# Both units of batch 0 through the FFN's weight pieces in three groups, with a new instruction order

## The chip, the cores and the metric

The kernel runs on one core of one Trainium2 chip. The metric is the device time of one execution in microseconds (us), as the median of several runs. PE is TensorE, DVE is VectorE, ACT is ScalarE, POOL is GpSimd and SP is SyncE, which issues nearly all transfers.

## The reference

```python
q, k, v: (4, 8, 576, 64)   moe_w_in: (512, 2048)   moe_w_out: (2048, 512)   all float32
q_rot, k_rot = rotate(q), rotate(k)                  # rotary embedding
scores = scale * q_rot @ k_rot^T
attn = exp(scores - rowmax);  attn = attn / (rowsum + 1e-9)
x = (attn @ v), heads side by side -> (2304, 512)
h = x @ w_in;  g = h * sigmoid(h);  out = g @ w_out
```

The result has to come close to that of float32, so nearly every matmul operand is split into a high and a low fp16 part with a scale, and products are made of three terms (high by high, high by low, low by high).

## The kernel before

**Attention.** Four batches, each with four head pairs p. For the first batch q and k are rotated in fp32 (three elementwise steps, `rope`, on DVE or POOL), transposed on PE (`qP`, L475 to L478), and evicted (`qE`, L484 on ACT, or L326 on DVE). A slot is 128 queries of one head: scores `S` (L915), negated row maximum `max` (L920, DVE), `exp` (L923, ACT), transposes `ET` (L928) and their eviction `EV` (L935 on ACT, L937 on DVE). `pv` (L982) multiplies with v. `RT` (L972) spreads the reciprocals of the row sums into the same PSUM bank as `pv`, `rn` (L987 on ACT, L326 on DVE) copies them out, `xn` multiplies. The other slots and batches work in split fp16 (L1034 and L1043 for `S`, L1077 for `exp`, `hi` and `lo` for the parts, L1145 for `pv`) and transpose the probabilities by DMA.

**Units.** A unit is 256 tokens of a batch (two blocks of 128 queries, all heads): units 0 and 1 are batch 0, units 2 and 3 batch 1, and so on to unit 7. The 64 tokens that each batch has left make up a last unit `rem`.

**Weights.** `w_in` and `w_out` come in eight pieces, one load or two for each matrix (`wld`), cleaned (`wT` L766 on ACT, `wC`, `wX`), their square sums taken (`wtr`, on PE or ACT) and added over the partitions (`wmm`, L819), from which a scale comes, and then split into high and low parts (`whi`, `wlo`). Raw pieces lie in a ring of three parts or in the places of later pieces.

**FFN.** A step (u, i) takes unit u through weight piece i: `m1` (L1200, 24 matmuls, PSUM tile m1 with one buffer), `tanh` (L1212), `g` (L1216), parts `gh` and `gl`, and `m2` (L1257), six matmuls for each of two 128-token tiles tt, which accumulate in one PSUM bank for each tile. After the last piece the bank is evicted with a scale (`o`) into the SBUF tile `ob`, and that is stored. All pieces share a scale over all weights (`wall`), and unit 0 alone is an exception: it starts before all pieces are loaded. Its pieces are in three groups (0 and 1; 2 to 4; 5 to 7). Each group has its own scale (`wgr`, `alpha_g`, `c_st`), accumulates in PSUM, and is evicted by `o` (written for the first group, added into `ob` on DVE for the others, L1270).

**Order.** The whole program is an order written out by hand: the string `ORDER` has one entry for each operation, its number in a list of names and the engine's letter (t PE, d DVE, a ACT, p POOL, s SP, A a transfer from ACT's queue, D a maximum with the scale fused in). Each engine takes its own entries in that order, so an operation that waits holds up all that stand behind it on its engine. A step needs the `xl` of all four head pairs of its unit, and its weight piece split.

```python
steps = [(u, i) for i0, n in GR for u in STREAM for i in range(i0, i0 + n)]
steps += [(u, i) for u in list(range(len(units))) + ["rem"] if u not in STREAM for i in range(NPC)]
...
if stream and i0:
    dve.scalar_tensor_tensor(out=t, in0=o, scalar=c_st[:, GI[i]:GI[i] + 1], in1=t, op0=ALU.mult, op1=ALU.add)
```

Of the kernel before, what the change touches and what calls it, by code (L numbers as in the profile page):

```python
# [48 lines left out]
549d 569d 580s 570a 571d 552t 553d 119p 748a 132s 554d 586p 572t 555d 558p 587d 581a 582a 573d 754t 755d 756a 759t
760d 1915d 574d 1909t 764t 765d 575d 1910a 761a 1912d 108d 583d 757t 758a 762t 766a 1922d 763a 556p 592a 1916t 594t  # L50
559p 595d 767t 593d 768a 1917d 596t 597d 598d 1923t 769t 557d 785t 69s 578a 599d 770d 602p 604a 1913p 1918t 786d 771a
787a 91s 777t 114d 603d 23s 576a 1919d 1920a 605d 577d 1921p 793t 778d 772a 67s 773d 1914d 1925t 1924a 1926d 630s 600a
779a 788a 789d 1927a 774a 631a 790a 606s 794d 801t 601d 802d 791d 579d 780a 632a 795a 781d 775d 120p 121s 1928p 98d
2013t 2014a 679d 782a 783p 803a 804a 607a 792s 825t 2015d 134a 796d 797d 2016a 141p 142p 115s 809t 147p 810d 811a 826d
133a 2020t 805d 148p 806a 610s 776s 784s 2017d 608a 807d 808s 827a 135t 817t 818d 136d 812d 2021a 609d 611a 2022d 612a
2023a 828d 2018t 613d 2019t 813d 614t 814p 2029t 626s 798a 799d 800s 615d 616a 137d 2024d 617d 618t 619d 819a 841t
2030a 620d 123s 149d 621d 138d 150a 2025t 815p 829d 109d 2031d 820d 622a 842d 843a 2032a 624a 830a 821d 627a 623d 816s
833t 834d 143p 857t 1929t 2027t 1930a 151d 858d 822a 831d 144p 145p 859a 1931d 2033d 823d 633d 628a 629d 634s 636a
# [1313 lines left out]
```

## Time and profile before

| | us |
|---|---|
| median of 3 runs | 638.02 |
| lowest and highest | 636.32, 639.64 |
| the profiled execution | 635.93 |
| its span, first to last instruction | 634.1 |
| PE, DVE, ACT, POOL busy in the span | 595.7, 473.4, 393.1, 325.4 |
| mean granted clock of PE | 0.976 |

The profile is of one execution. Busy times of an engine are the union of its instructions, and ends of matmuls are modelled. The granted clock is the share of PE's full 2.4 GHz; its other level, 1.2 GHz, reads 0.50. A mean duration of a group of instructions can exceed the distance between two of them, as an engine begins an instruction before the last one has ended.

### The profile page before, as it was taken

The numbers are of one execution on the slowest core, as the hardware profiler recorded it, in microseconds if no ns is written. First come the engines' busy times: TensorE is split into PE (matmuls) and PEld (weight loads), VectorE is DVE, ScalarE is ACT, GpSimd is POOL, SyncE is SP. The second block draws the span as 40 slices with busy tenths as digits, with TensorE's granted clock in tenths as the row PEclk, the third lists the DMA queues.
The fourth block names the chain that finished last, engine by engine and source line by source line (L and its number), as shares of the span: only waits on it lengthen the run. The fifth ranks groups of instructions, "written<-read, shape, count | busy, mean of one in ns | idle before, by whom it ended". The sixth has DMA issues, their size and how long they took to land.

```text
span 634.1 us, 12527 instructions
## 1 busy us (share of the span) xinstructions
PE 595.7 (94%) x4476; PEld 392.9 (62%) x4476; DVE 473.4 (75%) x1088; ACT 393.1 (62%) x816; POOL 325.4 (51%) x286
## 2 busy tenths in 40 slices
PE   0989887999999999999999999999999999999997
PEld 0657654566566656756666666666666676666663
DVE  2796877899999899978878998988799775322211
ACT  1576867998798776868777677666644633112322
POOL 2448244856566646554766256366754665221231
PEclk9975979989999999999999999999999999999999
DMA  6895506998989998989995897897965746200201
GB/s 177 258 318 212 158 2 156 230 242 173 178 177 176 171 181 158 150 170 172 173 208 122 137 173 150 162 193 141 155 111 96 129 80 124 51 1 1 51 2 33
DMA packets 210670, 91.17 MB, mean 144 GB/s; under 512 B 188464, under 2 KB 194352, under 8 KB 210608
## 3 DMA queue, kind: packets, MB, share of 16 engines
q1 hardware_dynamic: 209840, 89.36, 68.2%
q10 hardware_dynamic: 768, 1.02, 0.7%
q8 instruction: 35, 0.57, 0.4%
q14 instruction: 27, 0.22, 0.1%
HBM read 36.73 MB, written 4.72 MB: 65 GB/s over the span
## 4 chain that ended last, share of the span: by engine, by line
PE 79%; DVE 7%; DMA 6%; ACT 4%; SPq 2%; issue 1%; DVEq 0%; ACTq 0%
PE m L1200 28%; PE m L1257 26%; PE s L1043 7%; PE pv L1145 7%; PE s L915 2%; PE s L1034 2%; DMA Tq<-n 1%; DVE pn L338 1%; PE s L928 1%; PE s L1049 1%; DMA w_in<-in_v_dram 1%; DMA w_out<-in_moe_w_out_dram 1%; PE pv L982 1%; DMA w_out<-in_v_dram 1%; PE s L351 1%
## 5 line engine op out<-in xcount | busy, mean ns | idle before, releaser
L1200 PEld LDWEIGHTS <-w_in 128*128 128x128 f16 x1728 | 168.1, 99 | 33.9 <-issue 3.6
L1200 PE MATMUL m<-xh,w_in 128*128 128x256 f16 x1024 | 179.9, 274 | 0.3 <-DVE g L1216 0.3
L1257 PE MATMUL m<-w_out,gh 128*128 128x512 f16 x576 | 171.6, 379 | 0.0
L1200 PE MATMUL m<-xl,w_in 128*128 128x256 f16 x512 | 140.4, 274 | 0.0
L1077 ACT ACTIVATE e<-s,small 128x576 f32<-128x576 f32 x128 | 97.9, 765 | 62.2 <-DVE s L1059 18.4
L1257 PE MATMUL m<-w_out,gl 128*128 128x512 f16 x288 | 109.2, 379 | 0.2 <-POOL gl L341 0.2
L1216 DVE SCALAR_TENSOR_TENSOR g<-g,m 128x512 f32<-128x512 f32 x72 | 49.1, 682 | 70.0 <-ACT g L1212 39.4
L338 DVE SCALAR_TENSOR_TENSOR pn<-e,small,pn 128x576 f16<-128x576 f32 x94 | 85.9, 918 | 4.2 <-ACT pn L332 3.1
L1257 PEld LDWEIGHTS <-gh 128*128 128x128 f16 x576 | 51.8, 99 | 56.0 <-issue 5.1
L1212 ACT ACTIVATE g<-m,small 128x512 f32<-128x512 f32 x64 | 43.6, 682 | 51.4 <-PE m L1200 44.0
L1043 PE MATMUL s<-Tk,Tq 128*128 128x512 f16 (+1 forms) x384 | 60.8, 286 | 2.1 <-ACT e L1077 2.1
L332 ACT ACTIVATE pn<-e,small 128x576 f16<-128x576 f32 x69 | 52.4, 767 | 12.9 <-DVE small L1091 9.5
L1059 DVE TENSOR_SCALAR_CACHE_REDUCE s<-s,small 128x576 f32<-128x576 f32 x67 | 54.3, 816 | 2.0 <-PE s L1043 1.3
L326 POOL TENSOR_SCALAR g<-g,small 128x512 f32<-128x512 f32 x27 | 21.9, 811 | 64.8 <-ACT gh L332 30.7
L1145 PE MATMUL pv<-pt,vh 128*64 128x320 f16 (+1 forms) x504 | 54.1, 290 | 0.0
L326 POOL TENSOR_SCALAR e<-e,small 128x576 f32<-128x576 f32 x34 | 31.0, 911 | 39.6 <-ACT pn L332 16.9
L1257 PEld LDWEIGHTS <-gl 128*128 128x128 f16 x288 | 28.2, 98 | 34.6 <-POOL gl L341 0.7
L326 POOL TENSOR_SCALAR pn<-e,small 128x576 f16<-128x576 f32 x31 | 26.5, 854 | 41.5 <-DVE small L1091 31.5
L341 POOL TENSOR_TENSOR pn<-e,pn 128x576 f16<-128x576 f32 x34 | 45.4, 1335 | 2.8
L1043 PEld LDWEIGHTS <-Tq 128*128 128x128 f16 x384 | 28.3, 100 | 27.5 <-issue 7.0
L332 ACT ACTIVATE gh<-g,small 128x512 f16<-128x512 f32 x40 | 28.7, 718 | 16.5 <-DVE g L1216 11.9
L338 DVE SCALAR_TENSOR_TENSOR gl<-g,small,gh 128x512 f16<-128x512 f32 x45 | 35.7, 793 | 4.0 <-ACT gh L332 2.7
(212 smaller groups left out, 1057.8 us busy)
## 6 DMA issues: line engine op xcount, KB each, us to landing
w_out<-in_moe_w_out_dram SPq DMA_DIRECT2D x4, 1024.0 KB, 5.7
w_in<-in_moe_w_in_dram SPq DMA_DIRECT2D x4, 1024.0 KB, 6.5
out_dram<-ob SPq DMA_DIRECT2D x28, 128.0 KB, 2.4
io<-in_q_dram SPq DMA_DIRECT2D x12, 288.0 KB, 3.2
io<-in_k_dram SPq DMA_DIRECT2D x12, 288.0 KB, 3.7
io<-in_v_dram SPq DMA_DIRECT2D x12, 288.0 KB, 4.2
io<-in_v_dram SPq DMA_DIRECT2D x13, 256.0 KB, 4.5
ring<-in_moe_w_in_dram SPq DMA_DIRECT2D x3, 1024.0 KB, 5.8
```

Of the source, the lines that this page charges most:

```text
L326: e.tensor_scalar(out=out, in0=in0, scalar1=s1, scalar2=s2, op0=ALU.mult, op1=ALU.bypass if s2 is None else ALU.mult)
L332: act.activation(hi, src, AF.Copy, scale=s)
L338: dve.scalar_tensor_tensor(out=lo, in0=src, scalar=s, in1=hi, op0=ALU.mult, op1=ALU.subtract)
L341: e.tensor_tensor(out=lo, in0=src, in1=hi, op=ALU.subtract)
L1043: pe.matmul(o, tq[:, j, 2 * c:2 * c + 2, :], kt[:, r0:r1, js], start=(n == 0), stop=(n == 1))
L1059: dve.tensor_scalar(out=t, in0=t, scalar1=cc[1], scalar2=None, op0=ALU.mult, op1=ALU.min, accum_out=m_of(1, 2),)
L1077: act.activation(buf("e", i), buf("s", i)[:, 0:S], AF.Exp, bias=m_of(1, 2), scale=-1.0 if fused[i] else cc[0], accum_out=m_of(2, 3),)
L1145: pe.matmul(o[64 * j:64 * j + 64, 0:m], vt[part][:, j, s, :], pt[:, a, j, 0:m], start=(z == 0), stop=(z == len(steps) - 1),)
L1200: pe.matmul(t[:, c, 0:n], w[:, wz, kk, fs], xx[:, kk, 0:n], start=(kk == 0 and x == 0), stop=(kk == KD - 1 and x == 2),)
L1212: act.activation(g[:, :, 0:n], t[:, :, 0:n], AF.Tanh, scale=th_v[units[u][0]][:, i:i + 1])
L1216: dve.scalar_tensor_tensor(out=g, in0=g, scalar=1.0, in1=t, op0=ALU.add, op1=ALU.mult)
L1257: pe.matmul(o, gs[gz][:, c, ts], w[:, wz, c], start=(first and c == 0 and x == 0), stop=(last and c == 1 and x == 2),)
```

## The change

`STREAM` names the units that go through the weight pieces in groups. With unit 1 in it, unit 1 uses the scales of the groups (`alpha_g`, `c_st`) and no longer those over all weights, its two PSUM banks are evicted after pieces 1, 4 and 7, where they were evicted after piece 7 alone, and its second and third evictions add into `ob`. That makes four `o` operations more: 2,561 entries where there were 2,557. The numbers of the steps change, as the list of steps does (units 0 and 1 take turns by group in the list; where they stand in time is up to `ORDER`). `ORDER` is replaced as a whole: other places, and some 300 operations on another engine than before. One square sum, `wtr` of piece 0 of `w_out`, goes from PE to ACT.

```diff
-STREAM = (0,)
+STREAM = (0, 1)
...
-498s 500p 499a 4s 501d 1s 5d 2s 6d 7p 10p 11d 12d 26s 3s 8t 27d 28d 0d 13t 29p 494s 32d 9a 14d 495a 496a 15s 504t 689t
...
-727t 542a 544s 105d 80a 96d 728a 106d 678d 561a 107d 1902t 546a 97d 729t 739t 740d 741a 730d 731a 534p 734t 735d 589a
-1903d 736a 535d 1904t 742t 743a 100s 117p 732t 733a 1908d 564s 565a 1905d 591d 545a 737t 738a 563d 47s 749t 750d 751a
...
-1937d 2058t 918a 957D 919d 938t 139d 939D 940d 2062a 2063p 933a 958d 156t 912s 920s 959a 934d 2066t 157d 941a 947t
...
-185s 978d 967d 953a 2077t 964s 2078a 204d 197t 968a 198d 2079d 2080a 186a 205d 2071t 969d 184s 983t 984d 985d 979d
...
+498s 500d 0d 499a 4s 501d 1s 10d 2s 11d 504a 3s 12d 13t 5p 6d 7d 26s 494s 495a 32p 33p 8t 9d 505d 14a 689t 699t 496a
...
+725d 726a 80a 678d 590a 112p 727t 104t 105d 106d 729t 728a 730d 561a 589a 739t 544s 740d 734t 1904t 731a 537p 735d
+535d 741a 742t 562p 732t 736a 545a 117d 118d 98d 563d 737t 564s 743a 1902t 107d 591d 733a 1903d 542a 543d 584s 749t
...
+681d 2100d 2101a 910p 911p 912s 917d 918p 933a 957D 938t 958a 939d 940a 941a 919d 920s 2097t 2105t 139d 947t 140d
...
+936d 160a 161d 977a 162d 2103t 943d 2104t 2108p 978a 944p 1938t 1939a 209d 964s 1940d 965t 950a 195a 2029t 196a 197t
...
+193d 1030a 2042d 217a 1031a 1002d 2075t 2072d 225t 1032d 2043t 226d 999p 2076a 2077d 1033d 1015d 227t 232s 1003a 1004a
+1005a 228d 1006d 2078p 1007d 1073t 2079d 2073t 215A 218t 219d 229d 2044a 1019t 220d 1941t 1008p 230d 221d 1020D 231d
...
+2117a 1068a 1069d 2115s 1082t 1083D 2087t 2088d 1070a 238d 1084a 1085a 2118d 2119a 242p 1079a 1091t 1092D 1093a 1947t
+1086a 243p 244a 1071d 1100t 2123t 1101d 1087d 249p 2120d 1080d 1054s 2089t 245d 1948d 1094a 1095d 1072s 250a 2090d
```

The entries in these lines that matter, by what they are:

| operation | before | after |
|---|---|---|
| load of the first weight piece, `wld` of `w_in` | 494s | 494s |
| load of the identity; second load of q and k | 3s; 26s | 3s; 26s |
| rotation of q, three parts | 10p 11d 12d | 10d 11d 12d |
| transposes `qP` of q, of k | 13t, 8t | 13t, 8t |
| their evictions `qE` of q, of k | 14d, 9a | 14a, 9d |
| `wT`, `wC` of `w_in`, piece 0 | 495a, 496a | 495a, 496a |
| `wtr` of `w_out`, piece 0 | 504t | 504a |
| first scores `S` | 689t | 689t |
| `RT`, `rn`, `pv` of unit 0, pair 0 | 1902t, 1903d, 1904t | 1902t, 1903d, 1904t |
| `m1` of unit 0, piece 7; of unit 1, piece 0 | 2066t, 2077t | 2105t, 2029t |
| last `pv` of unit 1 ahead of it | 1938t | 1938t |
| new `o` of unit 1 after piece 1 | none | 2042d, 2044a |
| new `o` of unit 1 after piece 4 | none | 2088d, 2090d |

## Rows read from the trace of the kernel before

**Rows 1.** The page: span, busy time of the engines, PE's granted clock in 40 slices.

```profile
span 634.1 us, 12527 instructions
...
PE 595.7 (94%) x4476; PEld 392.9 (62%) x4476; DVE 473.4 (75%) x1088; ACT 393.1 (62%) x816; POOL 325.4 (51%) x286
...
PEclk9975979989999999999999999999999999999999
```

**Rows 2.** Busy time by stage: stretch, its us; PE, PEld, DVE, ACT, POOL; clock; DMA.

```profile
0.00:22.00 22.00, 6.16 (x34) 4.72 (x35) 7.20 (x10) 4.63 (x5) 7.79 (x10) 1.00 0.72 212
22.00:40.00 18.00, 14.00 (x105) 10.45 (x103) 16.21 (x40) 14.39 (x24) 8.79 (x6) 1.00 0.79 242
40.00:61.00 21.00, 20.54 (x83) 14.87 (x82) 15.33 (x33) 12.30 (x25) 13.94 (x13) 0.51 0.81 298
61.00:104.00 43.00, 35.67 (x241) 24.00 (x240) 32.66 (x64) 32.21 (x57) 17.59 (x16) 0.92 0.30 95
104.00:186.00 82.00, 77.56 (x532) 48.34 (x531) 74.80 (x172) 71.79 (x143) 50.53 (x38) 0.98 0.95 195
186.00:245.00 59.00, 58.23 (x485) 38.30 (x483) 54.66 (x137) 45.36 (x95) 36.16 (x31) 1.00 0.92 172
...
308.00:543.00 235.00, 234.77 (x1923) 154.30 (x1922) 193.61 (x463) 143.54 (x318) 137.49 (x127) 1.00 0.76 140
543.00:634.00 91.00, 86.37 (x590) 57.44 (x587) 22.08 (x34) 21.04 (x49) 17.58 (x20) 1.00 0.10 24
```

**Rows 3.** Timeline of the first 24 us: start, duration, engine, instruction, idle time before it.

```profile
10.00 0.59 SPq L442 DMA_DIRECT2D w_out<-in_q_dram  x1
...
11.46 0.76 DVE L462 TENSOR_TENSOR w_in<-w_in,cos_t 128x576 f32<-128x576 f32 x1 [1.18 <-DMA cos_t<-in_cos_dram]
...
13.58 0.58 SPq L425 DMA_DIRECT2D id_t<-in_ident_dram  x1
...
15.84 0.45 PE L475 MATMUL s<-id_t,w_in 128*128 128x128 f32 x1 [15.84 <-DMA id_t<-in_ident_dram]
...
18.46 0.65 ACT L484 ACTIVATE Tk<-s 128x576 f32<-128x576 f32 x1 [11.53 <-PE s L478]
...
19.29 0.42 PE L476 MATMUL s<-id_t,w_in 128*64 128x128 f32 x1
...
20.43 1.16 ACT L766 ACTIVATE w_in<-w_in 128x1024 f32<-128x1024 f32 x1 [1.31 <-DMA w_in<-in_moe_w_in_dram]
20.61 0.76 DVE L326 TENSOR_SCALAR Tq<-s 128x576 f32<-128x576 f32 x1 [1.75 <-PE s L478]
...
21.51 1.54 PE L915 MATMUL s<-Tk,Tq 64*128 64x64 f32 x10
...
23.39 0.27 PE L476 MATMUL s<-id_t,w_out 128*64 128x128 f32 x1
```

**Rows 4.** PE's waits: us in total, times, the longest.

```profile
PE s L1034 <- ACT e L1077: 4.8, 6, 2.4
PE s L928 <- ACT e L923: 3.5, 3, 1.7
...
PE pv L982 <- DVE pn L326: 1.5, 1, 1.5
```

**Rows 5.** DVE's groups by line and shape: busy us and mean ns of one.

```profile
L338 DVE SCALAR_TENSOR_TENSOR gl<-g,small,gh 128x512 f16<-128x512 f32 x45 | 35.7, 793 | 4.0 <-ACT gh L332 2.7 <-POOL gh L326 0.9
...
L338 DVE SCALAR_TENSOR_TENSOR n<-io,small,n 128x576 f16<-128x576 f32 x13 | 11.7, 904 | 0.3 <-ACT n L332 0.3
...
L338 DVE SCALAR_TENSOR_TENSOR w_out<-w_out,small 128x1024 f16<-128x1024 f32 x3 | 3.8, 1271 | 0.0
...
L1270 DVE SCALAR_TENSOR_TENSOR ob<-m,small,ob 128x512 f32<-128x512 f32 x4 | 2.9, 735 | 0.0
...
L937 DVE COPY pt<-s 128x640 f32<-128x640 f32 x2 | 1.6, 813 | 2.0 <-ACT e L923 2.0
...
L326 DVE TENSOR_SCALAR vh<-io,small 128x1152 f16<-128x1152 f32 x1 | 1.3, 1271 | 0.0
```

More of the change, by code (lines that the diff above doesn't have):

```diff
@@ L49 @@
[L49 to L58, printed above, removed]
@@ L159 @@
[L159 to L161 removed]
+498s 500d 0d 499a 4s 501d 1s 10d 2s 11d 504a 3s 12d 13t 5p 6d 7d 26s 494s 495a 32p 33p 8t 9d 505d 14a 689t 699t 496a
+497d 502a 27p 28p 15s 16t 29d 30t 48s 503d 690d 49d 17d 18t 19d 31a 59s 700d 506t 507d 60t 20d 704t 61d 62t 691a 692t
+508d 509d 50p 51d 81s 701a 54d 702t 510a 63d 693a 518s 64d 511d 21d 703a 82t 705d 37s 52t 83d 84t 520a 55d 85d 34p 22p
@@ new lines @@
+2368t 2369t 1693s 1998t 1764d 2371a 1755p 1741d 1735d 1742a 1743d 1722D 1723a 2372d 1744d 1724a 2373d 2374d 1999a
+1736p 1765s 1737p 1738s 1745p 1775t 1793t 2000d 1794d 1795d 1796a 1756s 1776d 2381t 1746d 1747s 1777d 2375t 2378t
+1725d 1726d 1778a 1779a 687d 2382a 1802t 1727d 1728p 1784t 1797a 2383d 1729s 2376a 1798d 1785D 2377s 1799a 2384p 1803D
+2379a 1786a 1780d 1800p 1781a 1801s 1782p 1783s 2388t 2385d 1804a 1805a 1806d 1807d 1787a 2389a 2390d 2386t 1808a
+1766t 1767d 1788d 1768d 1769a 1829t 1830D 1831a 1809p 1810s 1770d 2001t 1771d 1772d 2391p 2392d 1832a 1833d 1834d
@@ new lines @@
+2395t 1773d 2002a 1811t 2396a 2397d 2380s 1812D 1820t 2387t 1821d 1835a 1836d 1837s 1789d 1790p 2398d 2399d 1822a
+1823a 1824a 1825d 1813d 2402t 1814a 1791p 1792s 1838t 2403a 1847t 1848D 2393t 2394t 2404d 1849d 1826a 1850a 1827p
+1839D 1840d 1841a 1842a 2405p 2406p 1843d 1844a 1851d 2003d 1852d 1774s 2409t 2410a 2400t 2401t 1874t 1853d 1828s
+1845d 1892t 1875D 1893d 1815a 1846s 2411d 2412d 1894a 1876a 2004t 1854p 1816d 2407t 1817d 1855s 2408t 1895a 1896a
+1897d 1818d 1877a 1819s 1865t 2416t 2413d 2414t 1883t 1878a 1879d 1898a 1899d 1900s 1880d 1866D 1881p 2417a 2418d
@@ new lines @@
+1882s 2005a 1867d 1868a 1869d 2415t 1884D 1885d 2419a 2420p 2006d 1870d 1856t 1871p 1857D 1872d 1858a 1859a 1860a
+1886a 1861d 1862p 1887d 1863d 1864s 2423t 2424a 1873s 1888d 2425d 2421t 1889p 2007t 2008d 1890d 2430t 2426a 2427d
+2422t 2009d 2428t 2431a 1891s 2010t 2011a 2432d 2433a 2434p 2012d 2429t 2441t 2442a 2443d 2444d 2445d 2435t 2448t
+2449a 2436d 2438t 2450d 2451a 2452d 2439d 2446t 2455t 2440s 2447t 2453t 2456a 2457d 2458p 2462t 2459p 2454t 2460t
+2463a 2464d 2465d 2469t 2466d 2461t 2467t 2470a 2471d 2476t 2472d 2473p 2477a 2478d 2468t 2474t 2479d 2483t 2480d
@@ new lines @@
+2475t 2481t 2484a 2485d 2486p 2490t 2487d 2491a 2492d 2482t 2488t 2501t 2493d 2494p 2502a 2503d 2260s 2489t 2504p
+2495t 2496d 2508t 2505d 2509a 2498t 2510d 2506t 2515t 2499d 2500s 2507t 2511p 2512d 2317s 2513t 2516a 2517d 2518d
+2497s 2519d 2522t 2514t 2523a 2524d 2525d 2526d 2520t 2529t 2530a 2531d 2521t 2527t 2532a 2533p 2536t 2537a 2538d
+2528t 2534t 2437s 2543t 2539a 2540p 2535t 2544a 2541t 2545d 2546a 2550t 2547d 2551a 2542t 2552d 2548t 2553d 2549t
+2554d 2555t 2556a 2557s 2558t 2559a 2560s
```

200 lines of the change are left out of this document (92 added, 108 removed).

## The prediction

> **What bounds the kernel now.** I read the page's shares first, then busy time by stage, then the start instruction by instruction, then TensorE's waits, then the mean times of the kinds of instruction. The shares [rows 1] say that TensorE (PE) is busy 595.7 us of 634.1, DVE 473.4, ACT 393.1, POOL 325.4. A share over the whole span says little here, so the stages count [rows 2]. From 186 us to the end PE has work all the time (58.23 of 59, 234.77 of 235, 86.37 of 91, the last few us being the final eviction and store). The change can win next to nothing there; it can only lose by making PE wait. The time that can be won lies ahead of 186 us. PE is idle 15.8 us of the first 22, 4.0 of the next 18, 7.3 of 61 to 104 and 4.4 of 104 to 186, and its granted clock is 0.51 from 40 to 61 us and 0.92 from 61 to 104. DVE is the next engine in all of this: 54.66 of 59 us from 186 to 245, 74.80 of 82 before it.
>
> **What the change does.** First the promise. Unit 1 now keeps its sums in groups, so its first FFN step need no longer wait for scales over all weight pieces and could stand between the steps of unit 0. The new order does not use that. Read entry by entry, unit 1's first step (entry 2029, 2077 before) still stands behind unit 0's eighth step (2105, 2066 before), which needs the last weight piece. It could hardly stand earlier: it needs the attention output of its own unit, and in both orders the last pv of unit 1 comes one S ahead of it. On PE the row of steps and tiles is nearly the old one. No FFN work reaches the idle time ahead of 104 us, where the first step of unit 0 starts. So that part is worth 0, and it costs four more evictions. What is left is a shuffled order with some 300 instructions given to other engines. I cost it where I can.
>
> **Four more evictions and two that now add.** Unit 1 gets o at its second piece (one on DVE, one on ACT) and at its fifth (both on DVE), and both of its last ones add into SBUF on DVE. The eviction that adds takes 0.735 us [rows 5]. All fall between 186 and 245 us, where DVE has 59 - 54.66 = 4.3 us to spare [rows 2]. At the first seam PE has another S, a whole m1 step, a tile of m2 and two small matmuls between the tile that ends a group and the one that needs its bank; at the second seam, for the second tile, only two S and one tile of m2 (an S is two long matmuls here, an m2 tile of six is longer than one eviction). I take 0. Without that cover each seam would cost up to an eviction and its place in DVE's queue: four times 0.735 is 2.9, the upper bound. Nothing in it can be a gain.
>
> **The start.** The identity is now issued ahead of the second q and k load, not after it: at 10.00 rather than 13.58 us, and it landed 15.84 - 13.58 = 2.3 us after issue, so at 12.3 [rows 3]. All three rotations of q are on DVE: the second starts when cos is there (11.46), so q is ready at 11.46 + 2 x 0.76 = 13.0. PE's first transpose moves from 15.84 to 13.0, a gain of 2.8 us for PE. It is not kept. The first scores (S, L915) need the evictions of both transposes. Before, that of q was on DVE (20.61, 0.76) and S began at 21.51. Now it is on ACT (entry 14a), and ACT's queue holds wT of weight piece 0 in front of it (495a, L766), which waited until 20.43 for its load. That load keeps its place behind the same other loads, so ACT gets to the eviction at 20.43 + 1.16 = 21.6, takes 0.65 as the sibling at 18.46 did, and S starts at 22.24 + 0.14 = 22.4: 0.9 us later than before. What waits behind it on ACT are wC and the square sum of the same weight piece and then the first two exps, which I get some 3 us late; but ACT's list up to the fourth exp is no longer than before, so I carry +0.9, with 0 and +3 as ends.
>
> **PE's wait at the first pv.** RT and pv of the first head pair share a bank, and pv waited 1.5 us for DVE's copy of RT [rows 4]. In the new order RT (1902t) stands behind pv (1904t), so that wait goes. What is late next is the copy rn, needed by xn, which already had to wait for pv. I take -1.5, between -1.5 and 0.
>
> **Lighter DVE up to unit 1.** Counting both lists up to the first step of unit 1, DVE has lost 2 EV (0.813), 2 vhi (1.271), 1 wlo (1.271), 1 gl (0.793), and got 2 qlo (0.904) and 1 o (0.735) [rows 5]: -6.2 + 2.5. Other small kinds in both directions make -0.6 more, together -4.3 us out of the 186 us; by the first step of unit 2 it has got 4.8 back, so it is work put off. PE's waits in that part are for exps (4.8 us over six at L1034, 3.5 over three at L928) [rows 4], and an exp waits for DVE's maximum or for ACT's own queue, which has 0.8 us more by then. So a third of the 4.3 as gain: -1.4, ends -4.3 and 0. The 4.8 us that return in 186 to 245 meet 4.3 us of room: 0.5 us over, which PE may or may not feel.
>
> One square sum (wtr of piece 0) goes from PE to ACT, into time in which ACT waited for a load: 0. The weight loads that change places in the SP queue do so among themselves, and the DMA share is 0.30 from 61 to 104 us: 0. DMA transposes are as many as before.
>
> **Sum.** +0.9 - 1.5 - 1.4 + 0 = -2.0 us. The profiled execution took 635.93 us, 1.8 more than its span; less 2.0 this is 633.9. The median of the three runs, 638.02, is 2.1 above the profiled one, so I forecast **636.0 us**. A measurement of this kernel can tell some 0.5%, 3.2 us; this is inside.
>
> **The clock is what the sum leaves out.** PE's first transposes took 0.42 us each at 19.29, the same instruction 0.27 at 23.39 [rows 3]: PE began at 1.2 GHz and was at 2.4 after some 4 us of unbroken transposes. From 40 us it fell to 1.2 again for 21 us (0.51), after a stretch with PE busy 14.00 of 18 us [rows 2]. In the new order the unbroken transposes run from 13.0 to about 17.5, and then PE is idle until 22.4, where it was at work before.
> The Trainium skill (TensorE: Matmul & The Clock Gate, Part 1, "What's actually happening") says that the slow state is the default and that activity releases it; by that rule PE would meet 22.4 us in the slow state. The trace agrees at 15.84 and after.
>
> **Rivals.**
> *Slower: low clock from 22 us.* Place: 22 to 40 us. PE's 14.00 busy us double to 28 in 18 us of room if the whole stretch is at 1.2 GHz: +10. Each us of PE work done at the low clock adds one, and the 4.0 us of idle time take the first four, so it decides from 4 us of such work on. For it speaks the new hole; against it that PE then gets a denser run, after which the clock rose before. At 638.0 + 0.9 + 4 to 10, less the 2.9 above, 640 to 646; I write 643.
> *Faster: no low clock from 40 to 61 us.* If PE is granted the full clock late, in the thirties, and is dense then, it may keep it to 61. Its 20.54 us halve to 10.5; DVE's 15.33 of 21 bound the stretch: -5.7. With the sum this is 638.0 - 5.7 - 2.0 = 630.3, with part of it lost to ACT 633.
> *DVE becomes the bound in 186 to 245 us.* 0.5 to 2.9 us, 638.5: no change to be measured.
> *The change does nothing, as unit 1 comes no earlier, and the shuffle is neutral:* 638.0.
>
> **Chances.** Forecast 0.26; DVE bound or nothing at all 0.13; low clock from 22 us 0.26; high clock to 61 us, or the full -4.3 of the lighter DVE, 0.35. Within 0.5% (634.8 to 641.2) are the first two: 0.39. The range goes from 629 (the high clock's 630.3 less a spread of 1.5 us between runs) to 645 (10 us of low clock cut by one).
>
> **What would show it.** First transpose near 13 us, then a hole on PE to about 22.4 with ACT's L766 ahead of L484; no wait of PE at L982 for RT's copy; the first step of unit 0 within 3 us of 104 and of unit 1 within 5 us of 186; four more L1270 or L326 evictions, with PE still over 57 of 59 us in the stage of unit 1; the granted clock in 22 to 61 us, which decides between the rivals. I am wrong if PE shows waits for evictions of m2, or if the stage from 104 to 186 us, not the clock, has moved by more than 4 us.

## The result, and the profile after

The changed kernel takes **628.07 us** (median of 4 runs, 627.18 to 630.90) beside 638.74 for the kernel before in the same runs: ratio 0.985, 95% interval 0.980 to 0.989. It is faster by 1.5%; the forecast was 636.0 and the range ended at 629. The profiled execution took 628.26 us with a span of 626.5. Some executions take over 1.5% longer than the fastest of their kernel; ratios, intervals and "lost clock" leave them out here and below, medians do not.

The page, answering [rows 1]:

```profile
span 626.5 us, 12507 instructions
...
PE 589.8 (94%) x4468; PEld 389.6 (62%) x4468; DVE 475.9 (76%) x1087; ACT 396.1 (63%) x826; POOL 321.7 (51%) x279
...
PEclk9986999999999999999999999999999999999999
```

PE does the same work but for the square sum that moved to ACT (8 matmuls, 1.10 us before), and is busy 5.9 us less: it spends less time at the low clock. The clock's row has one dip left (8, 6) where before it had 7, 5 and later 7, 8. In the trace's clock records PE stood at 1.2 GHz from 40.5 to 61.0, 88.3 to 95.1 and 139.5 to 142.9 us before, and from 43.3 to 56.9 us now: 30.7 and 13.7 us. These records begin only at 20.0 us before and at 26.2 us now. Up to there the row reads full speed, but PE's transposes take 0.42 us each, as at 1.2 GHz, and 0.27 from there on. That is 4.2 us of PE's work before and 9.3 now, so the difference in work at the low clock is some 12 us and not 17. Busy time by stage, answering [rows 2]:

```profile
0.00:22.00 22.00, 5.06 (x21) 3.55 (x21) 6.52 (x9) 5.44 (x7) 7.94 (x9) 1.00 0.72 212
22.00:40.00 18.00, 17.42 (x113) 12.75 (x113) 16.04 (x38) 13.13 (x23) 9.82 (x7) 1.00 0.77 231
40.00:61.00 21.00, 19.50 (x91) 14.06 (x90) 16.38 (x36) 16.21 (x30) 15.10 (x12) 0.67 0.87 292
61.00:104.00 43.00, 39.23 (x286) 27.28 (x285) 40.63 (x79) 40.05 (x75) 22.44 (x19) 1.00 0.54 141
104.00:186.00 82.00, 75.68 (x544) 47.38 (x542) 79.75 (x172) 69.37 (x143) 50.15 (x38) 1.00 0.97 197
```

The stage from 61 to 104 us now holds 286 matmuls where it held 241, 79 DVE instructions for 64 and 75 ACT instructions for 57. From 104 to 186 DVE is busy 79.75 of 82 us (74.80 before): DVE has become the engine that is nearly always at work there. Where the time came from is best read at fixed points of the work, the start of one and the same PE instruction in both traces:

| PE starts | before | after | gained |
|---|---|---|---|
| first scores | 21.5 | 21.9 | -0.4 |
| scores of slot 4 | 40.9 | 40.0 | 0.9 |
| pv of pair 0 | 65.5 | 61.3 | 4.2 |
| scores of slot 16 | 90.3 | 83.1 | 7.2 |
| first FFN step of unit 0 | 103.7 | 93.0 | 10.7 |
| first FFN step of unit 1 | 185.7 | 175.5 | 10.2 |
| first FFN step of unit 2 | 245.1 | 237.0 | 8.1 |
| end of the span | 634.1 | 626.5 | 7.6 |

The whole gain, and 3 us more, is made ahead of the first FFN step; the stages of units 0 and 1 give some back. Each column is one execution, and executions of the same instructions differ. Up to the first FFN step e1, e4 and e16 (next section) run the instructions of the kernel before; they reach it at 102.8, 105.2 and 106.4 us. e2 and e3 run those of the kernel after and reach it at 95.0 and 92.9. From pair 0's pv to that step, however, the four old ones take 37.8 to 38.1 us and the three new ones 31.6 to 31.7, so that this distance tells smaller steps apart. That stretch before and after (in the columns of [rows 2]):

```profile
65.50:103.70 38.20, 32.31 (x219) 21.78 (x220) 28.85 (x56) 27.55 (x50) 15.43 (x14) 0.91 0.34 106
```

```profile
61.30:93.00 31.70, 30.02 (x224) 20.92 (x223) 29.69 (x60) 28.96 (x53) 16.54 (x14) 1.00 0.39 125
```

PE's idle time in it falls from 5.9 to 1.7 us, its busy time from 32.3 to 30.0. PE's waits over the whole span, answering [rows 4] (us in total, times, the longest):

```profile
PE s L915 <- ACT Tq L484: 3.6, 1, 3.6
PE m L1200 <- DVE g L1216: 2.6, 4, 1.4
...
PE s L928 <- ACT e L923: 1.4, 3, 0.8
...
PE s L1034 <- ACT e L1077: 0.4, 1, 0.4
```

The wait of pv for the copy of RT (1.5) is gone, and most of the waits for exp at L928 (3.5, now 1.4) and at L1034 (4.8, now 0.4). PE's timeline of the kernel before shows the waits in question, in its stretch from 61 to 104 us (start, duration, then in brackets the idle time ahead of it and who ended it):

```profile
65.53 2.53 PE L982 MATMUL pv<-pt,Tk 128*64 128x256 f32 x20 [1.48 <-DVE pn L326]
...
86.76 0.77 PE L928 MATMUL s<-id_t,e 128*128 128x128 f32 x5 [1.60 <-ACT e L923]
88.79 0.59 PE L819 MATMUL s<-small,ones 128*128 128x2 f32 x2 [1.26 <-ACT ring L807]
...
102.56 1.19 PE L1034 MATMUL s<-Tk,Tq 64*64 64x512 f32 x8 [2.42 <-ACT e L1077]
```

### The profile page after: what moved, and what is told of

Its sections match the earlier page's. It is cut to its first block, busy times and chain, and to the rows that moved or that the text cites. A ratio compares the mean times of both kernels' runs of the same rounds, so it can differ in the third digit from the quotient of the medians.

```text
span 626.5 us, 12507 instructions
## 1 busy us (share of the span) xinstructions
PE 589.8 (94%) x4468; PEld 389.6 (62%) x4468; DVE 475.9 (76%) x1087; ACT 396.1 (63%) x826; POOL 321.7 (51%) x279
## 4 chain that ended last, share of the span: by engine, by line
PE 72%; DVE 9%; ACT 7%; DMA 6%; issue 3%; POOL 2%; SPq 1%; ACTq 0%; DVEq 0%; POOLq 0%
PE m L1257 25%; PE m L1200 25%; PE pv L1145 7%; PE s L1043 7%; DMA pt<-pn 2%; DVE pn L338 1%; PE s L915 1%; DVE w_in L338 1%; ACT e L1077 1%; PE s L1049 1%; DVE small L1064 1%; DMA w_in<-in_moe_w_in_dram 1%; DMA w_in<-in_q_dram 1%; DMA io<-in_v_dram 1%; ACT e L923 1%
## 5 line engine op out<-in xcount | busy, mean ns | idle before, releaser
L1200 PEld LDWEIGHTS <-w_in 128*128 128x128 f16 x1728 | 166.2, 98 | 36.4 <-issue 7.2
L1200 PE MATMUL m<-xl,w_in 128*128 128x256 f16 x512 | 139.5, 273 | 0.9 <-POOL xl L1005 0.9
L338 DVE SCALAR_TENSOR_TENSOR pn<-e,small,pn 128x576 f16<-128x576 f32 x86 | 79.0, 921 | 9.7 <-ACT pn L332 6.4
L1212 ACT ACTIVATE g<-m,small 128x512 f32<-128x512 f32 x64 | 43.6, 681 | 61.3 <-PE m L1200 54.9
L332 ACT ACTIVATE pn<-e,small 128x576 f16<-128x576 f32 x71 | 53.9, 767 | 16.5 <-DVE small L1091 9.5
L326 POOL TENSOR_SCALAR e<-e,small 128x576 f32<-128x576 f32 x42 | 37.9, 902 | 46.5 <-DVE pn L326 34.1
L326 POOL TENSOR_SCALAR pn<-e,small 128x576 f16<-128x576 f32 x37 | 35.3, 955 | 46.7 <-DVE small L1091 21.5
L341 POOL TENSOR_TENSOR pn<-e,pn 128x576 f16<-128x576 f32 x42 | 57.4, 1366 | 3.5
L338 DVE SCALAR_TENSOR_TENSOR gl<-g,small,gh 128x512 f16<-128x512 f32 x52 | 43.2, 831 | 4.5 <-ACT gh L332 2.4
L326 POOL TENSOR_SCALAR g<-g,small 128x512 f32<-128x512 f32 x20 | 17.3, 865 | 52.9 <-ACT gh L332 35.2
L1145 PEld LDWEIGHTS <-vh 128*64 128x64 f16 x504 | 28.9, 110 | 12.2 <-issue 9.4
```

The source lines that it names most:

```text
L326: e.tensor_scalar(out=out, in0=in0, scalar1=s1, scalar2=s2, op0=ALU.mult, op1=ALU.bypass if s2 is None else ALU.mult)
L332: act.activation(hi, src, AF.Copy, scale=s)
L338: dve.scalar_tensor_tensor(out=lo, in0=src, scalar=s, in1=hi, op0=ALU.mult, op1=ALU.subtract)
L341: e.tensor_tensor(out=lo, in0=src, in1=hi, op=ALU.subtract)
L1145: pe.matmul(o[64 * j:64 * j + 64, 0:m], vt[part][:, j, s, :], pt[:, a, j, 0:m], start=(z == 0), stop=(z == len(steps) - 1),)
L1200: pe.matmul(t[:, c, 0:n], w[:, wz, kk, fs], xx[:, kk, 0:n], start=(kk == 0 and x == 0), stop=(kk == KD - 1 and x == 2),)
```

## Experiments

In the diffs an entry of the order is written by its name, with the letter of its engine (`RT.0.3t`: RT of unit 0, pair 3, on PE); "..." stands for other entries. Each run was timed beside the kernel before, whose median lay between 637.65 and 639.46 us. "Lost clock" is span times (1 - mean granted clock), the mean over a kernel's runs; it leaves out the start ahead of the first clock record, in the profiled executions 20.4 us of PE's work at the low clock in e8, 9.1 to 9.5 in after, e3 and e10, and 3.1 to 6.1 in the others. The columns on pv and FFN are of the profiled execution alone.

| kernel | us | ratio, 95% | first FFN step of unit 0, unit 1 | pv of pair 0 to first FFN step | lost clock |
|---|---|---|---|---|---|
| before | 637.65 to 639.46 | | 103.7, 185.7 | 38.1 | 16.9 |
| after | 628.07 | 0.980 to 0.989 | 93.0, 175.5 | 31.7 | 9.7 |
| e1 groups alone | 646.86 | 1.010 to 1.019 | 102.8, 187.9 | 37.9 | 20.3 |
| e2 order alone | 630.29 | 0.985 to 0.992 | 95.0, 177.3 | 31.7 | 13.0 |
| e3 new start, old rest | 632.93 | 0.991 to 0.997 | 92.9, 180.6 | 31.6 | 16.2 |
| e4 old start, new rest | 637.04 | 0.998 to 1.004 | 105.2, 189.1 | 38.1 | 15.6 |
| e5 new until slot 8 | 637.75 | 0.997 to 1.007 | 102.6, 186.8 | 36.7 | 16.9 |
| e6 new until slot 16 | 636.77 | 0.997 to 1.003 | 100.5, 184.8 | 39.2 | 18.7 |
| e7 RT of pair 0 | 632.85 | 0.989 to 0.996 | 99.7, 183.9 | 36.3 | 14.6 |
| e8 first scores earlier | 630.00 | 0.983 to 0.992 | 95.7, 180.1 | 31.6 | 9.4 |
| e9 RT of pairs 0, 3 | 635.64 | 0.991 to 0.998 | 96.0, 180.1 | 36.7 | 15.8 |
| e10 RTs put back | 632.89 | 0.991 to 0.997 | 97.2, 181.7 | 34.3 | 12.7 |
| e11 remainder on DVE | 633.52 | 0.992 to 0.999 | 98.5, 182.9 | 34.3 | 15.3 |
| e12 both | 633.06 | 0.990 to 0.997 | 100.4, 184.8 | 35.4 | 15.7 |
| e13 three waits | 632.72 | 0.991 to 0.998 | 97.2, 184.9 | 33.9 | 16.2 |
| e14 filler in before | 636.06 | 0.996 to 1.004 | 102.2, 188.7 | 37.8 | 11.3 |
| e15 filler in after | 626.04 | 0.980 to 0.989 | 92.9, 175.3 | 32.4 | 7.9 |
| e16 groups, later additions | 639.57 | 1.000 to 1.007 | 106.4, 191.1 | 37.8 | 17.4 |
| e17 e13 with a filler | 632.61 | 0.988 to 0.995 | 94.8, 182.2 | 31.2 | 14.3 |
| e18 before with it | 637.00 | 0.996 to 1.005 | 106.4, 190.9 | 39.5 | 16.1 |

### Which half of the change, and which part of the order

e1 has the old order with unit 1 in groups; e2 the new order without them.

```diff
 e1, old order:
-STREAM = (0,)
+STREAM = (0, 1)
-m2.0.1.1t ... m2.1.1.1t ... m2.0.1.4t ... m2.1.1.4t
+m2.0.1.1t o.1.1.0d ... m2.1.1.1t o.1.1.1a ... m2.0.1.4t o.1.4.0d ... m2.1.1.4t o.1.4.1d
 e2, new order:
-STREAM = (0, 1)
+STREAM = (0,)
-o.1.1.0d ... o.1.1.1a ... o.1.4.0d ... o.1.4.1d
```

Expected of e1: 

> The old order with unit 1 in three groups; its four new evictions stand right behind the tiles that end a group. If the grouping itself brings the gain, about 628. If it is the new order that does (my theory), this is at the kernel before, 638, or up to 2.9 us (four evictions of 0.735) above it: 638 to 641.

Expected of e2: 

> The new order without the grouping: unit 1 keeps its sums in PSUM over all eight pieces, and the four new evictions are left out. If the new order brings the gain, 626 to 629, as the changed kernel or a little below it. If the grouping is needed for it, about 638.

The groups alone cost 9 us, more than either forecast of e1 allowed; the new order alone gives what the whole change gives, within the intervals. From the first FFN step of unit 1 to that of unit 2 e2 takes 61.3 us and the kernel after 61.5: in the new order the four evictions cost nothing that can be seen.

e3 and e4 cut the order at the first FFN step, both without groups: e3 takes the new order up to there and then every other entry as the old order has it, e4 the reverse. e5 and e6 take the new order up to the scores of slot 8 or 16.

```diff
 e3:
-old order up to m1.0.0t, old order behind it
+new order up to m1.0.0t, old order behind it
 e4:
-old order up to m1.0.0t, old order behind it
+old order up to m1.0.0t, new order behind it
 e5, e6: as e3, up to S.8t, up to S.16t
```

Expected of e3: 

> The new order up to the first FFN step of unit 0, the old order for all that is left; no grouping of unit 1. The trace has that step start 10.7 us earlier in the changed kernel and the end 7.6 us earlier, so if the gain is made ahead of it, 627 to 630. If the order of the later stages matters, 634 to 638.

Expected of e4: 

> The old order up to the first FFN step of unit 0, the new order for all that is left; no grouping of unit 1. If the gain is made ahead of that step, 637 to 642 (the trace shows the new order giving back 3 us after it). If the later order brings the gain, 628 to 632.

Expected of e5: 

> The new order up to the scores of slot 8 (about 58 us), the old order behind it, no grouping. If the gain of the new start is the longer time at the high clock between 22 and 61 us, it is all here: 630 to 633. If it is the removed waits between 61 and 104 us, 636 to 638, as the trace has slot 8 only 2.7 us earlier.

Expected of e6: 

> The new order up to the scores of slot 16 (about 83 us), the old order behind it, no grouping. The trace of the changed kernel has that slot 7.2 us earlier. If the waits between 61 and 90 us carry the gain, 631 to 633; if what matters comes behind (the wait for exp at slot 20, 2.4 us), 634 to 636.

The new start is worth some 4 us by itself (e3's time lies between its two forecasts), the new rest nothing by itself, and the two together 7.4 (e2). e3 reaches the first FFN step as early as the kernel after does (92.9), but then needs 87.8 us to unit 1's first step, where after and e2 need 82.5 and 82.2. In that stage of e3 PE waits 2.7 us once for `g` and 2.2 in all for exp, and DVE waits 3.3 us for scores: an early start runs into an order made for a later one. That stage of e3 also has 10.2 us at the low clock, where after has none and e2 3.4; what the waits cost and what the clock costs there no run tells apart. e5 and e6 give nothing, although e6 is the new order up to slot 16 (its time lies above both forecasts): the old tail then puts RT of pair 3 ahead of slot 16, and PE waits 2.1 us for pair 3's reciprocals on DVE. So the entries from pair 0's pv to the first FFN step are needed. That those ahead of slot 8 are not is not shown: no run takes the old order up to there and the new one behind it.

e8 undoes the one thing that the change made later, the first scores.

```diff
-wT.0.in.0a ... qE.0.0.qa
+qE.0.0.qa wT.0.in.0a ...
```

Expected: 

> The changed kernel with the eviction of q ahead of wT of weight piece 0 on ACT. The first scores should start near 18.6 us and not 21.9. If the chain from the first scores sets the time, 625 to 626; if the weight piece behind it (wC, wX, the square sum) is what counts, 628, or worse where wT is now late.

First scores start at 18.9 instead of 21.9 us, and yet pair 0's pv comes at 64.1 and the time is 630.0, the second forecast. But PE's transposes take 0.42 us until 36 us in e8, and until 26 in the kernel after: here the earlier start came with a longer low clock, so what it is worth by itself is not shown.

### Single waits taken from the old order

e7 and e9 move RT behind a pv, in the kernel before; e11 takes a collision away; e12 does both, e13 one thing more.

```diff
 e7:
-RT.0.0t ... rn.0.0d ... pv.0.0t
+pv.0.0t RT.0.0t rn.0.0d
 e9, with the edit of e7:
-RT.0.3t S.16t ... pv.0.2t
+S.16t ... pv.0.2t RT.0.3t
 e11 (no move of RT):
-wlo.2.out.0p ... sc0.w.4d
+wlo.2.out.0d sc0.w.4d
 e12: e9 and e11
 e13, with e12:
-rn.0.3a ... whi.4.in.0a exp.17a
+exp.17a rn.0.3a ... whi.4.in.0a
```

Expected of e7: 

> The kernel before with one thing alone: RT of unit 0, pair 0 and its copy rn stand behind pv. My prediction put 1.5 us on it: 636. If PE only waits somewhere else instead, no change: 637.5.

Expected of e9: 

> The kernel before with three entries moved: TensorE's transpose of the reciprocals of pair 0 (and DVE's scaled copy of it) behind pair 0's pv, and that of pair 3 behind pair 2's pv. Theory A (the gain is made of single TensorE waits ahead of the first FFN step): pair 0's pv starts at 63.3 as in the run that moved pair 0 alone, the 1.26 us that TensorE stood ahead of slot 16 gets no shorter by the second move (it waited there for ACT, not for the transpose), but slots 16 and 18 are written 1.1 us earlier, and the 2.4 us wait for slot 16's exp at 102.6 shrinks by as much: 631 to 632.5 us. Rival B (only pair 0's wait mattered): 632.9, no better than that run.

e7 gives 4.7 us (2.6 to 6.8 by its interval) where the wait was 1.5, more than either forecast. In its profile pv waits no longer and the stretch behind it is 1.8 us shorter. e9 gives no more than e7, perhaps less: rival B. Slot 20's wait for exp stands in its trace as before (2.41 us), and piece 4's sum waits 2.1 us for ACT.

Behind the wait of 1.60 us at 86.76 stands the maximum of slot 15, and it is late because two of DVE's small operations take 1.28 and 2.12 us in the kernel before, where their like take 0.16. DVE, then POOL, in the kernel before:

```profile
81.59 1.28 DVE L962 TENSOR_SCALAR small<-small 128x4 f32<-128x4 f32 x1
82.92 0.18 DVE L963 RECIPROCAL small<-small 128x4 f32<-128x4 f32 x1
83.01 2.12 DVE L313 TENSOR_SCALAR small<-small 128x2 f32<-128x2 f32 x1
85.04 0.75 DVE L920 TENSOR_REDUCE small<-s 128x1 f32<-128x576 f32 x1
```

```profile
81.64 1.22 POOL L326 TENSOR_SCALAR w_out<-w_out,small 128x1024 f32<-128x1024 f32 x1
82.94 2.15 POOL L341 TENSOR_TENSOR w_out<-w_out 128x1024 f16<-128x1024 f32 x1
```

Each ends within 0.04 us of the end of a POOL instruction that began within 0.1 us of it. Their like take 0.16 us, so these two seem to have stood until POOL's was done. In the whole trace of the kernel before 14 of DVE's 388 small operations take over 0.3 us, and all 14 end within 0.04 us of the end of a POOL instruction. But some 200 others also begin while POOL is at work and are not held; what tells the two kinds apart stays open. e11 gives these two of POOL's instructions to DVE, as one, at a later place.

Expected: 

> The kernel before with one entry changed: the remainder of w_out's piece 2 goes from POOL (two instructions, 1.22 and 2.15 us, at 81.6 to 85.1) to DVE (one of 1.3 us), behind the maxima of slots 13 to 15 and ahead of piece 4's scales. Theory C (DVE's small operations of 0.16 us on SBUF alone stand while a POOL instruction on SBUF runs: 1.28 and 2.12 us in the kernel before, ending with POOL's two to within 0.05 us): L962 and L313 take under 0.4 us each in this stretch, slot 15's maximum comes 3 us earlier, slot 16 starts at 87.5 to 88 instead of 90.3, and the time falls by 2 to 4 us: 634 to 636. Rival D (they are slow for another cause, or exp on ACT holds the chain anyway): they stay above 1 us or slot 16 stays at 90, 637 to 639, the 1.3 us more on DVE being hidden or not.

The same lines of DVE in e11, and PE's at the wait:

```profile
81.87 0.16 DVE L962 TENSOR_SCALAR small<-small 128x4 f32<-128x4 f32 x1
82.07 0.18 DVE L963 RECIPROCAL small<-small 128x4 f32<-128x4 f32 x1
82.16 0.14 DVE L313 TENSOR_SCALAR small<-small 128x2 f32<-128x2 f32 x1
```

```profile
85.26 0.73 PE L928 MATMUL s<-id_t,e 128*128 128x128 f32 x5
86.33 0.38 PE L819 MATMUL s<-small,ones 128*128 128x2 f32 x2 [0.34 <-ACT ring L807]
```

0.16 and 0.14 us, the wait of 1.60 gone, that of 1.26 down to 0.34, slot 16 at 87.1 instead of 90.3 (22.9 us behind pair 0's pv instead of 24.7), and 633.5 us, by the ratio 3.1 us less (0.9 to 5.3): theory C holds here. The Trainium skill (GPSIMD Engine Reference, 1. Specifications) lists POOL's SBUF interfaces as shared with VectorE, with contention for VectorE's instructions in a two-port mode or with two inputs in SBUF; the trace agrees that the two engines hold each other up, by up to 2 us for an operation of 0.16; in which mode these operations ran it does not show.

Expected of e12: 

> The kernel before with the four entries of the two runs above together. If the gain of the change is these waits and no more (theories A and C together), slot 16 starts at 84 to 85, the first FFN step at 95 to 97, and the time comes to 629.5 to 631.5, at most 3 us above the kernel after. If the rest of the new order is needed (rival), it stays at 632.5 or more.

Expected of e13: 

> The kernel with pairs 0 and 3 behind their pv and piece 2's remainder on DVE (633.1 us), and one entry more: ACT's exp of slot 17 ahead of its scaled copy for pair 3 and its part of piece 4, which stood in front of it while slot 20 waited 2.4 us for it (in the kernel before too: 2.42 at 102.6). Theory A (the gain is single waits ahead of the first FFN step): slot 20's wait goes, the first FFN step comes 2 us earlier, 630.5 to 631.5. Rival F (the new order as a whole is needed: what goes at one wait comes back at the next): the wait ahead of slot 20 or of the first FFN step is found elsewhere, 632.5 to 634.

In time neither adds up: 633.1 and 632.7, the rivals both times. By the ratios e12 gives 4.2 us and e13 3.7, where e7 and e11 alone give 4.7 and 3.1; each of these is known to some 2 us only. Ahead of the first FFN step more of it is left: pv's wait (1.5) and the stretch behind pv together are 4.2 us shorter in e12, 5.7 in e13 and 7.9 in the kernel after than in the kernel before. In e13 the wait ahead of slot 20 is gone and the first FFN step comes at 97.2, but the next exp is no earlier, and PE waits there instead:

```profile
102.48 1.29 PE L1034 MATMUL s<-Tk,Tq 64*128 64x512 f32 x4 [1.65 <-ACT e L1077]
...
104.47 1.90 PE L1034 MATMUL s<-Tk,Tq 64*128 64x64 f32 x4 [0.70 <-ACT e L1077]
```

From the first to the second FFN step e13 takes 9.1 us, where before and after take 6.6 and 6.4. Part of what is taken away at one wait comes back at the next, as the order behind it was made for a later start.

e10 is the reverse: the kernel after, with the RTs put back.

```diff
-S.8t ... pv.0.0t ... RT.0.0t ... rn.0.0d ... S.16t ... pv.0.2t RT.0.3t
+RT.0.0t S.8t ... rn.0.0d pv.0.0t ... RT.0.3t S.16t ... pv.0.2t
```

Expected: 

> The kernel after with the transposes of the reciprocals put back where they stood before: pair 0's (with DVE's scaled copy) ahead of pair 0's pv, pair 3's ahead of slot 16. Theory A: TensorE waits ahead of pv 0 again (about 1.5 us) and stands some 1 to 2 us for pair 3's reciprocals on DVE ahead of slot 16, as the cut at slot 16 showed (2.1); with a longer stretch at the low clock behind it: 631 to 633 us. Rival B (the rest of the order hides them): 628 to 629, as the kernel after.

PE's waits from 60 to 100 us in e10:

```profile
PE mx L972 <- DVE pn L992: 2.1, 1, 2.1
...
PE pv L982 <- DVE pn L326: 0.7, 1, 0.7
```

2.8 us of waits are back (the second with 0.7 where 1.5 was forecast), the stretch behind pair 0's pv takes 34.3 us instead of 31.7, the first FFN step is 4.2 us later and the time 4.8 us longer (ratio to the kernel before 0.994, where it was 0.985). The places of these two entries are needed for about half of the gain.

### The clock

Over 105 runs of the kernel before, time follows lost clock: 0.70 us for each us lost, correlation 0.84. The kernel after loses 7.2 us less of it by the clock's records (9.7 against 16.9), and some 4.7 less with the start that they leave out (an estimate: half of 9.3 - 4.2 us off). Four kernels put transposes of the identity where PE waited, into columns of PSUM that nothing reads; they shorten no wait.

```diff
 e14 (before): 14 ahead of ET.3, 12 behind S.9, 13 ahead of ET.15, 10 ahead of wmm.4
 e15 (after): 9 behind S.4, 6 ahead of ET.13
 e17 (e13) and e18 (before): 13 behind ET.1
+            for z in range(13 if i == 1 else 0):
+                pe.transpose(t[:, 640:768], id_t, id_t)
```

Expected of e14: 

> The kernel before, in its order, with transposes of the identity into columns that nothing reads, where TensorE waited: 14 ahead of the transposes of slot 3's exp (a wait of 1.71 us), 12 behind the scores of slot 9 (1.48), 13 ahead of slot 15's (1.60), 10 ahead of piece 4's sum (1.26). They shorten no wait and add no work that anything needs. Theory E (the low clock follows TensorE's waits, and half of the gain is the clock): the stretches at 1.2 GHz that began at 40.5 and 88.3 go or come later, the lost clock falls from 17 to 8 to 12 us, and with 0.6 to 0.8 us of time for each the kernel takes 632 to 635 us. Rival G (the low clock doesn't hang on these waits): the same stretches, 637.5 to 640 us.

Expected of e15: 

> The kernel after, in its order, with 9 transposes of the identity behind the scores of slot 4 (TensorE then waits 1.06 us at 41.5) and 6 ahead of the transposes of slot 13's exp (0.77 us at 78.2). Theory E: the only stretch at 1.2 GHz, 43.3 to 56.9, goes or shrinks, 623 to 627 us, under both kernels. Rival G: the stretch stays, 628 to 629.5 us.

Expected of e17: 

> The kernel with three waits taken away in the old order (632.7 us, on average 17.5 us of clock lost per run), and 13 transposes of the identity behind the transposes of slot 1's exp, into columns that nothing reads, where TensorE waits 1.9 us (37.7 to 39.6) for slot 3's exp; ACT is in that exp until 39.5 and comes to slot 1's eviction only then, so that nothing waits for the filler. Theory E (the low clock from 40.3 to 60.8 follows TensorE's waits): the stretch goes, or ends some 10 us earlier; lost clock 8 to 13; the first FFN step 3 to 6 us earlier; 627.5 to 630.5 us, as the kernel after. Rival G (the low clock doesn't hang on this wait): stretch and time as without the filler, 632 to 634.

Expected of e18: 

> The kernel before with the same 13 transposes behind those of slot 1's exp and nothing else changed (in the kernel before TensorE waits 1.71 us there). Theory E: the stretch at 1.2 GHz that began at 40.5 and lasted 20.5 us goes or is halved, the lost clock falls from 17 to 8 to 13, and the time from 637.6 to 632 to 635. Rival G: 637 to 639.

e14 was badly made: a filler in the tile of an exp waits for that exp too, so that it ran behind the wait and not in it (the 13 at slot 15 began at 85.62, after PE had stood 1.53 us for the exp), and the 12 behind slot 9 kept its maximum waiting. Still, its runs lose less clock, 11.3 us against 16.9, as theory E said, and its time is that of the kernel before (0.9998). e17 and e18 have theirs in the wait. PE in e17, and the clock's row of e13 and of e17:

```profile
42.00 2.98 PE L930 MATMUL s<-id_t 128*128 128x128 f32 x13
44.77 0.82 PE L928 MATMUL s<-id_t,e 128*128 128x128 f32 x5
```

```profile
PEclk9975988979999999999999999999999999999999
```

```profile
PEclk9868998969999999999999999999999999999999
```

In e13 the clock is low from 40.3 to 60.8 us, in e17 from 38.2 to 45.0 (in e18 39.6 to 46.4). This can't be put down to the filler: the stretch of e17 and of e18 began before the filler did (42.00 and 43.55), and both had an earlier one (27.9 to 34.7 and 25.9 to 36.2) that e13 does not have. Such stretches move from execution to execution of the same instructions. Ahead of pair 0's pv they are 40.5 to 61.0 in the kernel before, 25.8 to 36.1 and 46.3 to 53.1 in e1, and 25.9 to 36.1 and 39.5 to 63.4 in e16. The clock lost per run is 14.3 us in e17 beside 16.2 in e13, and 16.1 in e18 beside 17.5 of the kernel before in the same runs, with a spread of 2.3 to 3.9 us between runs: not told apart. The times did not fall either: 632.6 beside 632.7, and a ratio of 1.0005, rival G. The filler itself ran at 1.2 GHz (2.98 us for 13) and took longer than the wait that it filled. e15's 626.0 us lies in theory E's range, but its ratio to the kernel before is the 0.985 of the kernel after, and in its profile the stretch from 43.3 to 56.9 us is gone and one as long stands from 21.1 to 34.8. So theory E's price for the low clock is not shown: no run here gained time by the clock alone.

At one place the profiles do tie the low clock to waits. In 11 of the 20 (before, e1, e4 to e7, e9, e10, e14, e16, e18) PE stands 1.5 us or more at one go shortly ahead of slot 16, as at 85.16 and 87.53 us in the kernel before. In all 11 the clock falls to 1.2 GHz there, while PE stands or up to 1.3 us later (88.3 in the kernel before). Of the nine without such a wait only e13 has a low stretch there. Ahead of slot 20 PE waits 2.4 us in 12 profiles, and in ten of them the clock stays up, so a wait alone does not decide it.

### Why the groups cost 9 us in the old order

In e1 DVE waits twice in unit 1's stage for PE's last product of the second group. DVE, then PE, in e1:

```profile
232.05 0.75 DVE L1270 SCALAR_TENSOR_TENSOR ob<-m,small,ob 128x512 f32<-128x512 f32 x1 [2.82 <-PE m L1257]
...
238.08 0.75 DVE L1270 SCALAR_TENSOR_TENSOR ob<-m,small,ob 128x512 f32<-128x512 f32 x1 [3.89 <-PE m L1257]
```

```profile
234.80 1.12 PE L1043 MATMUL s<-Tk,Tq 128*128 128x512 f16 x4 [2.79 <-ACT e L1077]
240.28 0.27 PE L1200 MATMUL m<-xh,w_in 128*128 128x256 f16 x1 [2.23 <-DVE g L1216]
```

DVE takes its instructions in order. While it stands for a product that PE has queued behind scores, the maximum queued behind it is not made, so exp is late, so PE's next scores wait for their buffer. e16 moves the two entries back in DVE's order.

```diff
-m2.0.1.4t o.1.4.0d max.53d ... m2.1.1.4t o.1.4.1d max.54D ... nr0.54a
+m2.0.1.4t max.53d ... m2.1.1.4t max.54D o.1.4.0d ... nr0.54a o.1.4.1d
```

Expected: 

> The old order with unit 1 in groups (646.9 us), with the two additions of the second group on DVE later in its order: behind the maximum of slot 54 and behind the small operations for slot 54. Theory H (the 9 us that the groups cost in the old order is DVE standing at these two additions for TensorE's last product of the group, 2.82 and 3.89 us, with the maxima that TensorE waits for queued behind): DVE's two waits fall under 1 us each, unit 1 takes 60 to 62 us instead of 67, and the time is 638.5 to 641. Rival I (it is the additions themselves, their work and the sums' buffers): 645 to 648.

DVE's waits for these products in unit 1's stage of e16, from the view of waits:

```profile
DVE ob L1270 <- PE m L1257: 0.4, 1, 0.4
```

Unit 1 takes 59.6 us instead of 67.4 (59.4 before), and the time is 639.6: theory H, but for some 2 us (0.1 to 4.6) by which it is still above the kernel before. In unit 1's stage the groups cost nothing where their additions stand behind the maxima that PE needs, and nearly 8 us where they stand ahead.

## Why the prediction was wrong

**The step that failed is the reading of what PE waits for ahead of the first FFN step, above all from 61 to 104 us.** The prediction saw that PE is idle 7.3 us there [rows 2] and then took one wait of it, pv's, and a third of DVE's lighter load for all the waits for exp. It let the waits of 1.60, 1.26 and 2.42 us stand as if the new order left them alone, and with the start's +0.9 the sum was -2.0 and the first FFN step "within 3 us of 104". It came 10.7 us earlier. Up to that step, and from there to unit 1's first, before and after (columns of [rows 2]):

```profile
0.00:103.70 103.70, 76.07 (x453) 53.76 (x454) 71.11 (x146) 63.23 (x108) 48.12 (x42) 0.87 0.58 186
103.70:185.70 82.00, 77.56 (x533) 48.35 (x532) 74.80 (x171) 71.79 (x142) 50.23 (x38) 0.98 0.95 195
```

```profile
0.00:93.00 93.00, 72.29 (x445) 51.28 (x445) 68.93 (x141) 64.05 (x110) 49.40 (x41) 0.93 0.65 205
93.00:175.50 82.50, 74.94 (x533) 47.01 (x531) 80.24 (x171) 71.40 (x146) 49.92 (x38) 1.00 0.97 196
```

PE's idle time up to the first FFN step falls from 27.6 to 20.7 us, which is 6.9 of the 10.7: waits that the new order takes away. Its busy time falls from 76.1 to 72.3, the other 3.8: the moved square sum and less work at 1.2 GHz. The clock was left out of the sum and stood among the rivals.

**PE's wait at the first pv: right mechanism, wrong size.** It is gone, as written. Its price was put at 1.5 us, its own length; alone it is worth 4.7 (e7). Only part of that is seen. In e7 the wait of 1.60 us is gone too, as the shift put POOL's instructions elsewhere against DVE's (L313 took 1.05 us there, not 2.12), but the one of 1.26 grows to 2.08. What made up the rest is not shown. The range of 0 to -1.5 left no room for this.

**Lighter DVE up to unit 1: wrong.** DVE's busy time up to unit 1's first step is 149.2 us now (68.93 to the first FFN step and 80.24 behind it) and was 145.9 (71.11 and 74.80). The prediction's count of instructions was to make it 4.3 us less (374 operations change engine, where it had some 300), but the same kinds take longer: L338 for `pn` 943 ns in the mean, 810 before. What changed is that DVE waits less: it is idle 26.3 us up to there, and was idle 39.8.

**Four more evictions: right in this order, wrong as a bound.** They cost 0 here (e2 against the kernel after; unit 1's stage is 2 us longer than before in both). The upper bound of 2.9 was the work of four evictions; placed badly they cost 9 us (e1), through what is queued behind them, not through their own time (e16).

**The start: right, and nothing is left of it by slot 4.** First transpose forecast 13.0, measured 13.29; first scores forecast 22.4, measured 21.9, behind ACT's L766 as described:

```profile
13.29 0.48 PE L475 MATMUL s<-id_t,w_in 128*128 128x128 f32 x1 [13.29 <-DVE w_in L465]
...
20.22 1.10 ACT L766 ACTIVATE w_in<-w_in 128x1024 f32<-128x1024 f32 x1 [10.65 <-DMA w_in<-in_moe_w_in_dram]
21.23 0.63 ACT L484 ACTIVATE Tq<-s 128x576 f32<-128x576 f32 x1
21.91 2.71 PE L915 MATMUL s<-Tk,Tq 64*128 64x64 f32 x8 [3.65 <-ACT Tq L484]
```

By slot 4 the 0.4 us are made good.

**The rivals.** *Low clock from 22 us*: begun, not kept up. The scores at 21.91 took 2.71 us for eight (1.54 for ten before), and PE's transposes 0.42 us until 26.1 and 0.27 from then on. It lasted 4 us and not the stage, in which PE was busy 17.42 of 18 us; the stage's granted clock reads 1.00, as the clock's records begin at 26.2 us, so here only the durations tell. That was luck in part: in e2, which runs the same instructions up to the first FFN step, the clock is low from 21.0 to 34.6 us, and that step comes at 95.0. By the rule of the Trainium skill that was quoted (TensorE: Matmul & The Clock Gate, Part 1, "What's actually happening") PE was to meet 22 us in the slow state; the trace agrees. *No low clock from 40 to 61 us* came nearest: 0.67 there instead of 0.51, and no low stretch later in this execution. *DVE becomes the bound from 186 to 245 us*: no, 52.90 of 59, and 55.30 of 61 in unit 1's stage, which is now 176 to 237; nearly so from 93 to 176, 80.24 of 82.5. *The change does nothing*: half right, as the groups do nothing and unit 1 follows unit 0 as before.

**What makes up the gain.** Shown: it is made by the order (e2), with the entries from pair 0's pv to the first FFN step needed for it (e3, e5, e6), about half of it hangs on the places of two RTs (e10), and it is kept in full only with the order behind (e3 against e2). In the old order two waits taken away give 4.7 and 3.1 us, and two or three together give 3.5 to 4.2, not more (e7, e11; e9, e12, e13), where the kernel after gives 9.8. Ahead of the first FFN step the order works more through PE's waits than through the clock, by two pairs of single executions. e13 and the kernel before have about as much PE work at 1.2 GHz ahead of the first FFN step, the start included (30.9 and 30.6 us), and e13 is there 6.5 us earlier; e2 and e1 have 27.8 and 25.3, and e2 is there 7.8 us earlier. Argued only: the rest, some 5 us between e13 and the kernel after, goes with the clock. Up to the second FFN step e13's profiled execution is 6.9 us behind (106.3 against 99.4), and it has run 9.5 us longer at half speed (32.5 us with its start, against 23.0), which would be worth some 4.8. The fall ahead of slot 16 is gone with the waits there. For the stretches ahead of pair 0's pv, which differ between executions of the same instructions, it stays open whether the order matters, and so does what the clock is worth: e14 lost 5.6 us less of it and took the same time.

## What to carry to other kernels

A wait removed is not worth its length: price it by the next fixed point of the work, and look at what it shifts against the other engines, for one of 1.5 us was worth 2.6 to 6.8 alone, and beside others no more could be told. Before a shift in one profile is put down to an edit, look how far it moves between executions of the same instructions. In an engine with a strict queue, an instruction that waits costs what stands behind it, not its own time; put what nobody is waiting for behind what somebody is. When an order is replaced as a whole, list every wait ahead of the first long dense stage in the old trace and look up each of its entries in the new order, before costing anything else.
